# Attention and routed experts on one core: order of the value loads, the memory rows, the casts and the noise load

## The chip, the cores and the metric

The kernel runs on one core of a Trainium2 chip. A core has a matrix engine (TensorE, PE in the profile, PEld for its weight loads), a vector engine (VectorE, DVE), an activation engine (ScalarE, ACT), a general engine (GpSimd, POOL) and SyncE (SP), which here only issues transfers. Transfers are started from the instruction queues of SP, ACT and GpSimd and carried by 16 DMA engines. The metric is the time of one execution on the device in microseconds, the median of several runs.

## What is computed

Four batches of 768 tokens with 8 heads of 64 go through chunked attention: each chunk of 32 queries sees 8 memory keys and a window of 16 tokens before it, its own 32 and 8 after it. The result, 3072 rows of 512, goes through a router that picks two of eight experts for each row, with noise in the choice.

```python
for c in range(nc):
    k_full = np.concatenate([mem_k, k[:, :, l_start:r_end]], axis=2)
    v_full = np.concatenate([mem_v, v[:, :, l_start:r_end]], axis=2)
    scores = scale * np.matmul(q_c, k_full.transpose(0, 1, 3, 2))
    a = np.exp(scores - np.max(scores, axis=-1, keepdims=True))
    out[:, :, c_start:c_end] = np.matmul(a / (np.sum(a, axis=-1, keepdims=True) + 1e-09), v_full)
...
noisy_logits = x @ w_gate + np.log1p(np.exp(x @ w_noise)) * noise
top2 = np.argpartition(-noisy_logits, 2, axis=1)[:, :2]
top2_w = softmax of the two logits
out[rows of e] += top2_w * (np.maximum(x @ w1[e], 0.0) @ w2[e])
```

Inputs are float32; the kernel computes in bfloat16 with float32 sums.

## The kernel before

There are two stages. The attention stage works through 12 tiles of 256 tokens, three to a batch (`i` counts tiles, `b` batches, `tp` the tile in its batch), and routes each batch while the next one runs. The expert stage then gathers rows of equal expert pairs and runs the two matmuls of each expert (`mm1`, L645, and `mm2`, L654). All eight experts' weights live in one large SBUF tile, `w_all`; the attention stage's buffers are cut from the end of the same tile, so a row of the profile that names `w_all` may be a weight or any of these buffers, and its line tells which.

Buffers of the attention stage: `k32`, `q32` and `v32` hold one batch of float32 keys, queries and values as they are loaded; `nat` holds keys and queries in bfloat16, two batches; `vb` holds the values in bfloat16, two batches. `vb` is laid out in groups of 64 rows on each of two halves of the partitions (`a` is 0 or 1, even and odd heads): 56 rows of a window and 8 memory rows, for 13 even groups and 12 odd ones, which are the same tokens moved by 32.

The steps that the change touches, with their engines and lines:

- `fetch` (L111): one transfer by SP's queue for a batch of keys or queries, 1536 KB.
- `fetch_v` (L119, L123, L127): a batch of values, 1536 KB, in twelve transfers by SP's queue, which alternate between the halves. For batch 0 it goes in two parts, groups below `VA` = 5 and the rest.
- `narrow` (L337): keys or queries to bfloat16; by ScalarE and VectorE for batch 0, by GpSimd after that (`cp_p`, L479 in the profile).
- `cast_v` (L314): values to bfloat16 on 64 partitions, by GpSimd, except one by VectorE in batch 0.
- `shift_v` (L322, L323): two transfers by SP's queue that make a half's odd groups from its even ones.
- `memory_v` (L333 for batch 0, L330 after it): the memory rows `mvn` into eight partitions of each half, by SP's queue. It must wait until the shifts have read the places that it overwrites.
- `turns` (L346 and L473): transposes of keys (`KU`) and queries (`QU`) on TensorE with copies by ScalarE and VectorE.
- `scores` (L357 to L375), `exps` (L380), `turn_p` (L387, L390), `values` (L398 to L413), `turn_x` (L421, L423), `gate` (L433, L435): the work on a tile. `values` needs the cast groups, the shifted groups and the memory rows.
- `keep_x` (L440): the tile's rows to HBM, by GpSimd's queue for the first seven tiles, by SP's after that.
- `route` (L231 to L311): a generator of eight steps for a batch. Each `next` records one: exponentials (1), first choice (2, L240 to L251), second choice (3, L256 to L264), ranks on TensorE and `d` on GpSimd (4, L267 to L288), `vals` on GpSimd (5, L296), ranks read (6), `oh_l` (7, L304), lists (8, L308, L310).
- `load_expert`, `load_part` (L74, L75, L81, L83): expert weights by GpSimd's queue. Each waits until the buffers that it overwrites are free.

For PE, ACT, DVE and SP the order of instructions is that of the program text (`manual_schedule`). On GpSimd each instruction that is given to `pin` keeps its place. Every queue works in order: an instruction that waits holds all behind it. SP's transfers take eight semaphores in turn, so a transfer is issued only when the eighth before it has landed.

In a middle batch of the kernel before, tile 0 narrows the next batch's keys and fetches the keys after that; tile 1 does the same for queries and casts half 0 of the values; tile 2 casts half 1, and SP's queue then has the shifts, the values of the batch after next, and the memory rows, in this order:

```python
if tp == 2:
    for a in range(2):
        shift_v(b + 1, a)
    if b + 2 < B:
        fetch_v(b + 2)
    memory_v(b + 1)
```

The noise `nz` is loaded by SP's queue ahead of tile 0 (L503). The casts of the memory values `mvn` (L162) and of the gate weights `wgn` (L168) are VectorE's work before the first key transposes.

Of the kernel before, what the change touches and what calls it, by code (L numbers as in the profile page):

```python
# [22 lines left out]
def kernel(  # L23
# [14 lines left out]
    nc = tc.nc  # L38
    B, H, S, D = q.shape
    NM = mem_k.shape[2]  # L40
    CH, LC, RC = 32, 16, 8
# [28 lines left out]
    def pin(i):  # L70
        tc.keep_in_program_order(i)
# [37 lines left out]
    def fetch(x, b):  # L109
        t, a = {"k": (k32, k), "q": (q32, q)}[x]  # L110
        nc.sync.dma_start(out=t, in_=a[b].rearrange("h (p s) d -> p h (s d)", s=SO))  # L111


    def fetch_v(b, g0=0, g1=NB):
        src = [v[b].rearrange("(c a) t d -> a t c d", a=2)[a] for a in range(2)]
        t = [v32[a * 64:a * 64 + 64] for a in range(2)]
        if g0 == 0:
            for a in range(2):
                nc.sync.dma_start(out=t[a][LC:64, 0], in_=src[a][0:64 - LC])  # L119
        lo, hi = max(g0, 1), min(g1, NB - 1)  # L120
        for c in range(HP):
            for a in range(2):
                nc.sync.dma_start(out=t[a][:, lo:hi, c],  # L123
                                  in_=src[a][lo * 64 - LC:hi * 64 - LC, c].rearrange("(g p) d -> p g d", p=64))
        if g1 == NB:
            for a in range(2):
                nc.sync.dma_start(out=t[a][0:LC, NB - 1], in_=src[a][S - LC:S])  # L127


    for g in (0, NB - 1):  # L130
# [1 line left out]
    fetch("k", 0)  # L132
    fetch("q", 0)
    VA = 5
    fetch_v(0, 0, VA)

    actx = ExitStack()
    keep = actx.enter_context(tc.tile_pool(name="keep", bufs=1))
# [19 lines left out]
    mvs = wflat[0:NM, 0:2 * B * Dm].bitcast(F32).rearrange("m (b h d) -> m b h d", b=B, h=H)  # L158
    nc.scalar.dma_start(out=mvs, in_=mem_v.rearrange("b h m d -> m b h d"))
    mvn = keep.tile([NM, B, Dm], BF16, name="mvn")  # L160
    for b in range(B):
        nc.vector.tensor_copy(mvn[:, b].rearrange("m (a c d) -> m a c d", a=2, c=HP),  # L162
                              mvs[:, b].rearrange("m (c a) d -> m a c d", a=2))
    wgs = keep.tile([128, KP, 2 * E], F32, name="wgs")
    nc.scalar.dma_start(out=wgs[:, :, 0:E], in_=moe_w_gate.rearrange("(kp p) e -> p kp e", p=128))
    nc.scalar.dma_start(out=wgs[:, :, E:2 * E], in_=moe_w_noise.rearrange("(kp p) e -> p kp e", p=128))
    wgn = const.tile([128, KP, 2 * E], BF16, name="wgn")
    nc.vector.tensor_copy(wgn, wgs)  # L168
    nz = const.tile([128, NG, E], F32, name="nz")
# [143 lines left out]
    def cast_v(b, a, g0, g1, eng):  # L313
        i = eng.tensor_copy(out=vb[b % 2][a * 64:a * 64 + 64, a, g0:g1],  # L314
                            in_=v32[a * 64:a * 64 + 64, g0:g1].rearrange("p g c d -> p g (c d)"))
        if eng is nc.gpsimd:
            pin(i)


    def shift_v(b, a, g0=0, g1=NB - 1):  # L320
        t = vb[b % 2][a * 64:a * 64 + 64, a]
        nc.sync.dma_start(out=t[0:32, NB + g0:NB + g1], in_=t[32:64, g0:g1])  # L322
        nc.sync.dma_start(out=t[32:WIN, NB + g0:NB + g1], in_=t[0:WIN - 32, g0 + 1:g1 + 1])  # L323

    def memory_v(b, g0=0, g1=NB - 1):
        for a in range(2):
            t = vb[b % 2][a * 64 + WIN:a * 64 + KW, a]
            m = mvn[:, b, a * HP * D:(a + 1) * HP * D].unsqueeze(1)
            if g1 - g0 == NB - 1:
                nc.sync.dma_start(out=t, in_=m.to_broadcast([NM, 2 * NB - 1, HP * D]))  # L330
# [150 lines left out]
    with tc.manual_schedule(engines={ET.PE, ET.Activation, ET.DVE, ET.SP}):  # L481


        for x, us in ((0, KU), (1, QU)):
            narrow(x, 0, 0, cp_a)
            narrow(x, 0, 1, cp_v)
            turns(0, us, [cp_a, cp_v])
        cast_v(0, 0, 0, VA, nc.gpsimd)
        cast_v(0, 1, 0, VA, nc.vector)
        for a in range(2):  # L490
            shift_v(0, a, 0, VA - 1)
        fetch_v(0, VA)
# [12 lines left out]
        for i in range(NT):  # L505
            b, tp = divmod(i, TP)
            more, last = b + 1 < B, b + 1 == B
            r = routes.get(b - 1)
            if i:
                keep_x(i - 1, nc.gpsimd if i < NT - 4 else nc.sync)  # L510
            if tp == 2 and r:
                next(r)
            if more:
                if tp < 2:
                    for par in range(2):
                        narrow(tp, b + 1, par, cp_p)
                    if b + 2 < B:
                        fetch("kq"[tp], b + 2)
                if tp:
                    cast_v(b + 1, tp - 1, 0, 7, nc.gpsimd)  # L520
                    cast_v(b + 1, tp - 1, 7, NB, nc.gpsimd)
                if tp == 2:
                    for a in range(2):
# [6 lines left out]
            if i == NT - 4:  # L530
                load_expert(1)
            if i == NT - 3:
                load_part(2, 0)
                load_part(2, 1)
# [6 lines left out]
            if i == NT - 1:  # L541
                next(r)
                next(r)
            if i:
                xTs_[i - 1] = turn_x(xrs.pop(i - 1))
            pTs[i] = turn_p(pbs.pop(i))
            if i:
                gate(i - 1, xTs_.pop(i - 1))
            if i + 1 < NT and not held:
                pbs[i + 1] = exps(sc)  # L550

            if tp == 0 and b:
                r = routes[b - 1] = route((b - 1) * SO, SO, lgs[b - 1])
                next(r)
            if tp and r and i < NT - 1:
                next(r)
# [36 lines left out]
        src = next(dec)  # L593
# [296 lines left out]
```

## Time and profile before

| | us |
|---|---|
| median of 3 runs | 440.17 (437.24 to 440.24) |
| time of the profiled execution | 440.2 |
| its span, first to last instruction | 438.5 |
| PE busy | 304.6 |
| DVE busy | 173.7 |
| POOL busy | 150.1 |
| ACT busy | 126.8 |
| first routed rows asked for by GpSimd (L608) | 199.55 |
| expert matmuls back to back from | 216.76 |

The page's second part cuts the span into 40 slices of 11 us. Its digits are tenths of a slice in which an engine was busy; PEclk is the clock that TensorE was granted, in tenths; DMA is the mean busy share of the 16 DMA engines.

```profile
PE   0433183035717654533799999999999999999990
DVE  6563044028617563874212332167431133202230
POOL 9303436016526710236840653206152022100021
PEclk9965575556665655555899999999999999889997
DMA  8546889976481999202999997062121012100011
```

To the left of the eighteenth slice is the attention stage: no engine is busy throughout, and TensorE is nearly idle in slices 7 to 9 (66 to 99 us). To the right, from slice 20 on, TensorE is busy all the time. A row of the groups reads: line, engine, operation, output and inputs, count, then busy time and mean duration, then the idle time of the engine just before these instructions and what ended most of it.

### The profile page before, as it was taken

The numbers are of one execution on the slowest core, as the hardware profiler recorded it, in microseconds if no ns is written. First come the engines' busy times: TensorE is split into PE (matmuls) and PEld (weight loads), VectorE is DVE, ScalarE is ACT, GpSimd is POOL, SyncE is SP. The second block draws the span as 40 slices with busy tenths as digits, with TensorE's granted clock in tenths as the row PEclk, the third lists the DMA queues.
The fourth block names the chain that finished last, engine by engine and source line by source line (L and its number), as shares of the span: only waits on it lengthen the run. The fifth ranks groups of instructions, "written<-read, shape, count | busy, mean of one in ns | idle before, by whom it ended". The sixth has DMA issues, their size and how long they took to land.

```text
span 438.5 us, 7981 instructions
## 1 busy us (share of the span) xinstructions
PE 304.6 (69%) x3315; PEld 192.7 (44%) x3315; DVE 173.7 (40%) x362; ACT 126.8 (29%) x193; POOL 150.1 (34%) x180
## 2 busy tenths in 40 slices
PE   0433183035717654533799999999999999999990
PEld 0423073034606543422455544667446666445540
DVE  6563044028617563874212332167431133202230
ACT  2330153015424441310243223422224312024310
POOL 9303436016526710236840653206152022100021
PEclk9965575556665655555899999999999999889997
DMA  8546889976481999202999997062121012100011
GB/s 236 125 104 196 208 129 356 177 182 190 99 142 30 156 230 218 58 24 73 185 242 210 229 215 172 24 99 81 43 81 50 0 38 87 43 1 3 17 49 55
DMA packets 59320, 53.29 MB, mean 122 GB/s; under 512 B 32455, under 2 KB 51703, under 8 KB 59280
## 3 DMA queue, kind: packets, MB, share of 16 engines
q0 software_dynamic: 16912, 28.71, 30.6%
q1 hardware_dynamic: 40776, 23.85, 23.1%
q8 instruction: 28, 0.46, 0.4%
q10 hardware_dynamic: 1592, 0.16, 0.3%
q14 instruction: 12, 0.10, 0.1%
HBM read 56.49 MB, written 10.75 MB: 153 GB/s over the span
## 4 chain that ended last, share of the span: by engine, by line
PE 49%; DVE 3%; DMA 2%; POOL 1%; issue 1%; POOLq 0%; ACT 0%; DVEq 0%
PE p_y L654 24%; PE p_h L645 23%; DMA xt<-xd,main_src 2%; PE p_xt L626 1%; POOL xt L608 1%; DVE w_all L413 0%; DVE oh_l L304 0%; PE p_list L308 0%; PE p_x L421 0%; POOL facts L285 0%; PE ps_o L405 0%; POOLq L845 0%; DVE y L660 0%; DVE listed L310 0%; PE p_xt L760 0%
## 5 line engine op out<-in xcount | busy, mean ns | idle before, releaser
L654 PE MATMUL p_y<-w_all,h 128*128 128x512 bf16 (+1 forms) x464 | 107.0, 387 | 0.0
L645 PE MATMUL p_h<-xTt,w_all 128*128 128x384 bf16 (+2 forms) x640 | 103.1, 321 | 0.0
L645 PEld LDWEIGHTS <-w_all 128*128 128x128 bf16 (+1 forms) x704 | 68.5, 99 | 42.5 <-issue 3.7
L633 ACT ACTIVATE h<-p_h 128x512 bf16<-128x512 f32 (+1 forms) x82 | 44.7, 545 | 112.6 <-PE p_h L645 105.7
L631 DVE TENSOR_SCALAR h<-p_h 128x512 bf16<-128x512 f32 (+1 forms) x50 | 31.3, 626 | 97.0 <-PE p_h L645 90.1
L654 PEld LDWEIGHTS <-h 128*128 128x128 bf16 x464 | 45.7, 100 | 53.1 <-issue 3.8
L612 POOL DMA_INDIRECT out_dram<-y,main_dst x28 | 30.9, 1105 | 103.8 <-DVE y L660 90.4
L405 PE MATMUL ps_o<-w_all,pT 128*32 128x128 bf16 x384 | 12.4, 295 | 53.4 <-DMA w_all<-mvn 53.4
L413 DVE TENSOR_TENSOR w_all<-ps_o,rs 128x512 bf16<-128x512 f32 x24 | 15.5, 686 | 59.6 <-PE ps_o L405 59.1
L660 DVE SCALAR_TENSOR_TENSOR y<-p_y,main_w,y 128x512 f32<-128x512 f32 x28 | 21.0, 750 | 37.4 <-PE p_y L654 35.1
L608 POOL DMA_INDIRECT xt<-xd,main_src x28 | 27.4, 977 | 23.6 <-PE p_xt L626 15.4
L405 PEld LDWEIGHTS <-pT 128*32 128x32 bf16 x384 | 9.1, 131 | 54.2 <-issue 39.3
L314 POOL CAST w_all<-w_all 64x1792 bf16<-64x1792 f32 (+3 forms) x15 | 23.5, 1591 | 26.7 <-DMA w_all<-mvn 13.4
L423 ACT COPY xT<-p_x 128x1024 bf16<-128x1024 bf16 x12 | 12.2, 1015 | 69.8 <-PE p_x L421 69.8
L658 ACT ACTIVATE y<-p_y,main_w 128x512 f32<-128x512 f32 x28 | 19.2, 687 | 42.2 <-PE p_y L654 41.2
L346 PE MATMUL p_t<-identb,w_all 128*128 128x128 bf16 x192 | 20.9, 295 | 9.6 <-DVE mkT L229 3.5
L346 PEld LDWEIGHTS <-w_all 128*128 128x128 bf16 x192 | 18.3, 137 | 11.3 <-ACT w_all L337 5.7
L479 POOL CAST w_all<-w_all 128x1536 bf16<-128x1536 f32 x12 | 17.2, 1465 | 12.8 <-DMA w_all<-in_k_dram 8.0
L440 POOL DMA_DIRECT2D xd<-w_all x7 | 5.3, 763 | 41.3 <-DVE ps_s L370 35.0
L626 PE MATMUL p_xt<-identb,xt 128*128 128x128 bf16 x116 | 10.3, 235 | 8.8 <-DMA xt<-xd,main_src 8.0
L373 DVE TENSOR_REDUCE mx<-ps_s 128x16 f32<-128x1024 f32 x12 | 14.7, 1224 | 3.6 <-PE ps_s L363 3.3
L380 ACT ACTIVATE pb<-sc 128x1024 bf16<-128x1024 f32 x12 | 12.7, 1061 | 10.9 <-DVE sc L375 10.9
(160 smaller groups left out, 311.7 us busy)
## 6 DMA issues: line engine op xcount, KB each, us to landing
w_all<-in_moe_w_dram POOLq DMA_DIRECT2D x10, 1024.0 KB, 14.7
w_all<-in_k_dram SPq DMA_DIRECT2D x4, 1536.0 KB
w_all<-in_q_dram SPq DMA_DIRECT2D x4, 1536.0 KB
w_all<-in_moe_w_dram POOLq DMA_DIRECT2D x12, 512.0 KB, 8.4
w_all<-in_v_dram SPq DMA_DIRECT2D x24, 176.0 KB
xd<-w_all POOLq DMA_DIRECT2D x7, 256.0 KB, 5.0
xd<-w_all SPq DMA_DIRECT2D x5, 256.0 KB
w_all<-w_all SPq DMA_DIRECT2D x6, 192.0 KB
```

The source lines that it names most:

```text
L314: i = eng.tensor_copy(out=vb[b % 2][a * 64:a * 64 + 64, a, g0:g1], in_=v32[a * 64:a * 64 + 64, g0:g1].rearrange("p g c d -> p g (c d)"))
L346: nc.tensor.transpose(out=p_t[:, s, :], in_=src[:, pair, s, :], identity=identb)
L405: nc.tensor.matmul(out=ps_o[r * CH:(r + 1) * CH, j, 2 * pair:2 * pair + 2, :], lhsT=pT[:, j * HP + pair, r * CH:(r + 1) * CH], rhs=vb[b % ...
L479: pin(nc.gpsimd.tensor_copy(o_, i_))
L608: pin(nc.gpsimd.indirect_dma_start(out=xts[key].bitcast(I32), out_offset=None, in_=xd, in_offset=bass.IndirectOffsetOnAxis(ap=ix, axis=0)))
L612: i = nc.gpsimd.indirect_dma_start(out=out, out_offset=bass.IndirectOffsetOnAxis(ap=ix, axis=0), in_=y, in_offset=None, bounds_check=N - 1 ...
L631: nc.vector.tensor_scalar(out=out_, in0=in_, scalar1=0.0, scalar2=None, op0=Alu.max)
L633: nc.scalar.activation(out=out_, in_=in_, func=Act.Relu)
L645: nc.tensor.matmul(out=o, lhsT=w(kp * F + f * 128, 128), rhs=x[:, kp], start=(kp == 0), stop=(kp == KP - 1))
L654: nc.tensor.matmul(out=p, lhsT=h[:, (f * n + j) * 128:(f * n + j + 1) * 128], rhs=w(KP * F + f * Dm, Dm), start=(f == 0), stop=(f == FB - 1))
L658: nc.scalar.activation(out=y, in_=p, func=Act.Copy, scale=weight)
L660: nc.vector.scalar_tensor_tensor(out=y, in0=p, scalar=weight, in1=y, op0=Alu.mult, op1=Alu.add)
```

## The change

The values of the next batch are cast at tile 1 of batch 0 and at tile 0 of every later batch, both halves together, instead of over tiles 1 and 2. The queue of SP then has the shifts, a load of keys or queries, the memory rows, and only after them the values of the batch after next. Values are fetched one half after the other. In batch 0 the memory rows of the first part stand between the two halves of the second part of the values, and those of the second part behind the keys of batch 1 but in front of the queries. Narrowing of keys and queries and their fetches move by about a tile. In `route`, the second choice (3) comes behind the tile's values, `vals` (5) follows at tile 1, and the ranks and `oh_l` (6, 7) come ahead of the next scores. Expert weights are asked for one tile later. The noise goes by GpSimd's queue at the start; the casts of `mvn` and `wgn` move behind the first value cast and the first scores.

```diff
-    def fetch_v(b, g0=0, g1=NB):
-        src = [v[b].rearrange("(c a) t d -> a t c d", a=2)[a] for a in range(2)]
-        t = [v32[a * 64:a * 64 + 64] for a in range(2)]
+    def fetch_v(b, a, g0=0, g1=NB):
+        src = v[b].rearrange("(c a) t d -> a t c d", a=2)[a]
+        t = v32[a * 64:a * 64 + 64]
...
-    for b in range(B):
-        nc.vector.tensor_copy(mvn[:, b].rearrange("m (a c d) -> m a c d", a=2, c=HP),
-                              mvs[:, b].rearrange("m (c a) d -> m a c d", a=2))
...
-    nc.vector.tensor_copy(wgn, wgs)
     nz = const.tile([128, NG, E], F32, name="nz")
+    pin(nc.gpsimd.dma_start(out=nz, in_=moe_noise.rearrange("(g p) e -> p g e", p=128)))
...
-        for x, us in ((0, KU), (1, QU)):
-            narrow(x, 0, 0, cp_a)
-            narrow(x, 0, 1, cp_v)
-            turns(0, us, [cp_a, cp_v])
+        narrow(0, 0, 0, cp_a)
+        narrow(0, 0, 1, cp_v)
+        turns(0, KU, [cp_a, cp_v])
+        narrow(1, 0, 0, cp_a)
+        narrow(1, 0, 1, cp_v)
+        turns(0, QU, [cp_v, cp_a])
         cast_v(0, 0, 0, VA, nc.gpsimd)
         cast_v(0, 1, 0, VA, nc.vector)
+        for b in range(B):
+            nc.vector.tensor_copy(mvn[:, b].rearrange("m (a c d) -> m a c d", a=2, c=HP),
+                                  mvs[:, b].rearrange("m (c a) d -> m a c d", a=2))
         for a in range(2):
             shift_v(0, a, 0, VA - 1)
-        fetch_v(0, VA)
+        fetch_v(0, 0, VA)
         memory_v(0, 0, VA - 1)
-        fetch("k", 1)
+        fetch_v(0, 1, VA)
+        pbs[0] = exps(scores(0))
+        nc.vector.tensor_copy(wgn, wgs)
         for a in range(2):
             cast_v(0, a, VA, NB, nc.gpsimd)
-        pbs[0] = exps(scores(0))
+            shift_v(0, a, VA - 1)
+        fetch("k", 1)
+        memory_v(0, VA - 1)
+        fetch("q", 1)
         for a in range(2):
-            shift_v(0, a, VA - 1)
-        fetch("q", 1)
-        memory_v(0, VA - 1)
-        fetch_v(1)
-        nc.sync.dma_start(out=nz, in_=moe_noise.rearrange("(g p) e -> p g e", p=128))
+            fetch_v(1, a)
+        for par in range(2):
+            narrow(0, 1, par, cp_p)
         routes = {}
         for i in range(NT):
...
+            if more and tp == min(b, 1):
+                for par in range(2):
+                    narrow(1, b + 1, par, cp_p)
+                if b == 0:
+                    fetch("k", 2)
+                elif b + 2 < B:
+                    fetch("q", b + 2)
+            if more and tp == 1 - min(b, 1):
+                for a in range(2):
+                    cast_v(b + 1, a, 0, 7, nc.gpsimd)
+                    cast_v(b + 1, a, 7, NB, nc.gpsimd)
+                    shift_v(b + 1, a)
+                if b + 2 < B:
+                    fetch("k" if b else "q", b + 2)
+                memory_v(b + 1)
+                if b + 2 < B:
+                    for a in range(2):
+                        fetch_v(b + 2, a)
+            if b + 2 < B and tp == 2:
+                for par in range(2):
+                    narrow(0, b + 2, par, cp_p)
+            if i == NT - 4:
+                load_expert(0)
+            if i == NT - 3:
+                load_expert(1)
+            if i == NT - 2:
+                load_part(2, 0)
+                load_part(2, 1)
             if tp == 2 and r:
                 next(r)
-            if more:
-                if tp < 2:
-                    for par in range(2):
-                        narrow(tp, b + 1, par, cp_p)
-                    if b + 2 < B:
-                        fetch("kq"[tp], b + 2)
-                if tp:
-                    cast_v(b + 1, tp - 1, 0, 7, nc.gpsimd)
-                    cast_v(b + 1, tp - 1, 7, NB, nc.gpsimd)
-                if tp == 2:
-                    for a in range(2):
-                        shift_v(b + 1, a)
-                    if b + 2 < B:
-                        fetch_v(b + 2)
-                    memory_v(b + 1)
-            if i == NT - 5:
-                load_expert(0)
...
+                next(r)
...
-            if tp and r and i < NT - 1:
-                next(r)
+            if tp == 1 and r:
                 next(r)
...
             xrs[i] = values(i, pTs.pop(i))
+            if tp == 1 and r:
+                next(r)
             if tp == 1 and more:
                 turns(b + 1, KU, [cp_a])
+            if tp == 1 and r:
+                next(r)
+                next(r)
...
-            if tp and r and i < NT - 1:
+            if tp == 2 and r and not last:
                 next(r)
```

More of the change, by code (lines that the diff above doesn't have):

```diff
@@ L111, in fetch @@
         nc.sync.dma_start(out=t, in_=a[b].rearrange("h (p s) d -> p h (s d)", s=SO))
-    def fetch_v(b, g0=0, g1=NB):
-        src = [v[b].rearrange("(c a) t d -> a t c d", a=2)[a] for a in range(2)]
-        t = [v32[a * 64:a * 64 + 64] for a in range(2)]
+    def fetch_v(b, a, g0=0, g1=NB):
+        src = v[b].rearrange("(c a) t d -> a t c d", a=2)[a]
+        t = v32[a * 64:a * 64 + 64]
         if g0 == 0:
-            for a in range(2):
-                nc.sync.dma_start(out=t[a][LC:64, 0], in_=src[a][0:64 - LC])
+            nc.sync.dma_start(out=t[LC:64, 0], in_=src[0:64 - LC])
         lo, hi = max(g0, 1), min(g1, NB - 1)
         for c in range(HP):
-            for a in range(2):
-                nc.sync.dma_start(out=t[a][:, lo:hi, c],
-                                  in_=src[a][lo * 64 - LC:hi * 64 - LC, c].rearrange("(g p) d -> p g d", p=64))
+            nc.sync.dma_start(out=t[:, lo:hi, c],
+                              in_=src[lo * 64 - LC:hi * 64 - LC, c].rearrange("(g p) d -> p g d", p=64))
         if g1 == NB:
-            for a in range(2):
-                nc.sync.dma_start(out=t[a][0:LC, NB - 1], in_=src[a][S - LC:S])
+            nc.sync.dma_start(out=t[0:LC, NB - 1], in_=src[S - LC:S])
     for g in (0, NB - 1):
@@ L134 @@
     VA = 5
-    fetch_v(0, 0, VA)
+    for a in range(2):
+        fetch_v(0, a, 0, VA)
     actx = ExitStack()
@@ L510 @@
                 keep_x(i - 1, nc.gpsimd if i < NT - 4 else nc.sync)
+            if more and tp == min(b, 1):
[14 more added lines that the diff above has]
+                if b + 2 < B:
+                    for a in range(2):
+                        fetch_v(b + 2, a)
[9 more added lines that the diff above has]
+                load_part(2, 1)
             if tp == 2 and r:
                 next(r)
-            if more:
-                if tp < 2:
-                    for par in range(2):
-                        narrow(tp, b + 1, par, cp_p)
-                    if b + 2 < B:
-                        fetch("kq"[tp], b + 2)
-                if tp:
-                    cast_v(b + 1, tp - 1, 0, 7, nc.gpsimd)
-                    cast_v(b + 1, tp - 1, 7, NB, nc.gpsimd)
-                if tp == 2:
-                    for a in range(2):
-                        shift_v(b + 1, a)
-                    if b + 2 < B:
-                        fetch_v(b + 2)
-                    memory_v(b + 1)
-            if i == NT - 5:
-                load_expert(0)
[L530 to L534, printed above, removed]
+                next(r)
             held = i == TP - 1
@@ L540 @@
                 sc = scores(i + 1)
-            if i == NT - 1:
-                next(r)
-                next(r)
             if i:
```

1 line of the change is left out of this document (removed).

## The prediction

> **What bounds the kernel now.** The profiled execution has a span of 438.5 us and a time of 440.2, so 1.7 us lie outside the span; the median of the three runs is 440.17, and the sum below is made against 440.2. I read the chain that ended last first: from 216.8 us to 428 it is matmuls of the expert stage back to back, which the change does not touch. Before that it goes through the gather of rows and the routing of the last batch, so the expert stage begins when the attention stage ends, and what the attention stage waits for counts in full. The page's costliest groups name that wait:
>
> ```profile
> L654 PE MATMUL p_y<-w_all,h 128*128 128x512 bf16 (+1 forms) x464 | 107.0, 387 | 0.0
> L645 PE MATMUL p_h<-xTt,w_all 128*128 128x384 bf16 (+2 forms) x640 | 103.1, 321 | 0.0
> ...
> L405 PE MATMUL ps_o<-w_all,pT 128*32 128x128 bf16 x384 | 12.4, 295 | 53.4 <-DMA w_all<-mvn 53.4
> ```
>
> The two expert lines wait for nothing. The values matmul (L405) works 12.4 us and waits 53.4, all of it for the memory rows (mvn). TensorE's timeline shows where, namely at the first values of each batch, and at tile 1:
>
> ```profile
> 36.21 0.29 PE L405 MATMUL ps_o<-w_all,pT 128*32 128x128 bf16 x1 [5.65 <-DMA w_all<-mvn]
> ...
> 53.96 0.27 PE L405 MATMUL ps_o<-w_all,pT 128*32 128x128 bf16 x1 [8.30 <-DMA w_all<-mvn]
> ...
> 94.27 1.04 PE L405 MATMUL ps_o<-w_all,pT 128*32 128x128 bf16 x32 [20.63 <-DMA w_all<-mvn]
> ...
> 132.88 1.04 PE L405 MATMUL ps_o<-w_all,pT 128*32 128x128 bf16 x32 [9.91 <-DMA w_all<-mvn]
> ...
> 170.01 1.16 PE L405 MATMUL ps_o<-w_all,pT 128*32 128x128 bf16 x32 [8.02 <-DMA w_all<-mvn]
> ```
>
> I call these five starts T0, T1, T3, T6 and T9 after their tiles. Why the rows come late stands in SP's queue ahead of T3:
>
> ```profile
> 70.48 0.78 SPq L323 DMA_DIRECT2D w_all<-w_all  x1
> 71.32 1.05 SPq L119 DMA_DIRECT2D w_all<-in_v_dram  x2
> 72.41 13.14 SPq L123 DMA_DIRECT2D w_all<-in_v_dram  x8
> 85.59 1.54 SPq L127 DMA_DIRECT2D w_all<-in_v_dram  x2
> 87.18 1.54 SPq L330 DMA_DIRECT2D w_all<-mvn  x2
> ```
>
> The shifts of batch 1 are issued by 71.3, but its memory rows only at 87.2, behind twelve transfers of batch 2's values. The same stands ahead of T6 (values 116.3 to 126.3, rows at 126.4). At T9 no load is left to queue behind; there the rows land beside expert weights.
>
> **Prices of the transfers.** Stretches with one kind of transfer (last two columns: DMA share, GB/s):
>
> ```profile
> 81.00:87.00 6.00, 0.00 (x0) 0.00 (x0) 0.00 (x0) 0.00 (x0) 0.00 (x0) 0.50 1.17 174
> 103.00:106.00 3.00, 0.00 (x0) 0.00 (x0) 2.65 (x11) 0.88 (x2) 0.86 (x3) 0.50 1.03 383
> 128.00:132.00 4.00, 0.00 (x0) 0.00 (x0) 0.00 (x0) 0.00 (x0) 0.00 (x0) 0.50 0.34 44
> 116.00:118.00 2.00, 1.73 (x44) 1.45 (x44) 1.84 (x5) 0.93 (x1) 0.00 (x0) 0.50 0.83 183
> ```
>
> So one batch costs the engines: values, 1536 KB at 174 GB/s, 9.0 us; keys or queries, 1536 KB at 383, 4.1 each; memory rows, 200 KB at 44, 4.7; the shifts, 336 KB per half at 183, 1.8 a half. Transfers of SP go through in the order of issue, as the row of 87.2 shows, and SP keeps eight in flight at most (they take eight semaphores in turn).
>
> **The change, part by part.**
>
> *T0.* VectorE's cast of the gate weights (L168) now stands behind the first scores; before, VectorE idled 3.0 us in front of it, with the key copies behind. The query load's landing takes the place of part of this: I take 2 us of the 3. Shift a=1 then ends at 23.9 instead of 25.9. Five value transfers instead of ten (5.40 + 1.08, halved: 3.2) come before the first memory rows: 27.1. Issuing those takes 3.0, and 1.4 to land (35.5 to 36.97 before): 31.6 for the second half, 31 for the first matmul. The mvn casts (four, 1.72) go onto VectorE behind the value cast and end by 26, under SP's issuing; without that cover T0 would be 1.7 later.
>
> The noise load goes from SP to GpSimd's queue at about 10 us. GpSimd is idle from 13.1 to 19.3, so its issue costs nothing (one to two us bound it, by the 0.7 to 0.9 of its other DMAs). Its 96 KB took 62 to 65 us on the engines, at 44 GB/s; I count between 0 and 3 us on the first loads, take 1, and T0 is 32. The Trainium skill ("DMA: Bandwidth & Descriptors", section "Issuing engines are not separate DMA queues") says that queues of different engines share the DMA engines and interleave, and that only issue time is saved; by it alone the 3 us would move rather than go, and the sum would be 2 us higher. The trace shows the queues sharing the DMA engines (195 GB/s in all where expert weights and rows ran together), not this move.
>
> *T1.* Five value transfers (3.2) end at 35; the second half lands at 35.5, its GpSimd cast (1.92) ends at 37.5, its shift's issue (1.55) at 39, keys of batch 1 at 39.5. The rows must wait for the shifts to land and come behind the keys (4.1): they land at 46. Before, keys and queries both were in front, and T1 was 54.
>
> *T3.* Now it is a row of transfers from 46: queries 4.1, values of batch 1 9.0, keys of batch 2 4.1, shifts 3.6, queries of batch 2 4.1, rows 4.7: 29.6, hence T3 = 75 instead of 94.3. TensorE would be ready for it at about 66 (queries narrowed on GpSimd at 52, turned, and 12.1 us from the values of tile 2 to those of tile 3 as before), so some 9 of the 20.6 us of waiting remain: T3 has its load of values out of the way, not its keys and queries.
>
> *T6.* Behind the rows come batch 2's values (9.0): 84. GpSimd now casts them ahead of keep_x and of the queries of batch 2: cast a=1 (3.09) 87.1, keep_x 0.75, narrow (2.87) 90.7. Queued behind this on GpSimd are the routing's d and vals; TensorE waits for the narrow with its query turns. From those to T6 it was 108.06 to 132.88 less 9.91, that is 14.9: T6 = 105.6. Its rows: shift 88.7, keys 4.1, rows 4.7, landed at 98, so that no wait is left. Compute alone gives 75 + 28.7 = 103.7; I take 105.6.
>
> *T9.* Compute from T6 was 37.1 less 8.02, 29.1: 134.7. Supply: values of batch 3 at 107, cast 110, queries 111.5, narrow 114.5, plus 14.9 is 129.4. TensorE decides, T9 = 134.7 instead of 170.0, 35.3 earlier.
>
> *Behind T9.* Same work as before (270.2 us). The expert loads (L74, L75, L81) move by one or two tiles and now start near 120 in one row; they took 143 to 177 before, so they end near 154, ahead of the gather at 164. If that cover were gone, the first expert matmul would wait, up to 10 us. The routing's reordered VectorE steps do the same work; the two-input ones can stall beside GpSimd:
>
> ```profile
> L240 DVE TENSOR_TENSOR nl<-ns,nz x5: 174/199/4195, 99.5 to 192.4; 128x48 f32<-128x48 f32 x3, 128x32 f32<-128x32 f32 x1, 128x16 f32<-128x16 f32 x1
> ```
>
> 199 ns as a rule, 4.2 us twice (99.5 and 138.1), each time until GpSimd's casts were through. I leave both stalls in.
>
> Sum: 440.2 - 35.3 = 405, own range 397 to 412.
>
> **Rivals.**
>
> *More goes.* The stalls of 4 us vanish in batches 1 and 2, for the value casts leave that place, and T3 comes 4 us earlier with rows and keys overlapping: 405 - 8 - 4 = 393. For it: only the query narrow (2.87) still stands beside L240. Against: GpSimd's cast wait moves the narrow to just there.
>
> *GpSimd and VectorE collide more.* Per batch the casts (6.2) and the narrow (2.9) now come in one stretch; if all 9 us fell on two-input steps in place of 4, and in front of T6 and T9, that is 2 x 5: 415. The Trainium skill ("GPSIMD Engine Reference", section "Key points") says that GpSimd shares its SBUF interfaces with VectorE and contends with instructions of two SBUF inputs; by that rule this is the outcome, and the two rows of 4.2 us agree with it.
>
> *Little changes.* The rows still stand behind keys or queries, and a late cast only exchanges the wait: only T0 and T1 gain, 8 us, 432. Against it: 9.0 us of values leave the row ahead of both T3 and T6.
>
> *Slower.* The halves (64 partitions each) now go one after the other instead of by turns. If a half fills the engines no better than the eight-partition rows (44 GB/s, share 0.34), values take 36 us, not 9. They stand once in the supply row ahead of each of T3, T6 and T9, so T9 becomes 129 + 3 x 27 = 210 and the time 480. It decides for slower from 23 us a batch (68 GB/s). Against: the 32-partition shifts already reach 183.
>
> **Chances and range.** Forecast 0.60, more 0.17, collision 0.12, little 0.06, slower 0.05. A measurement of this kernel can tell about 1% (4.4 us) from no change. All but the last are faster by more; of "little" I give 0.02 to within 1%. So 0.93 faster, 0.02 same, 0.05 slower. The range runs from 393 to 419, over forecast, more and collision and 4 us past that for the noise load and the half loads.
>
> **What would show it.** In the changed profile L405's waits should fall from 53.4 to some 20 us, with T0, T1, T3, T6, T9 near 32, 46, 75, 106, 135, no wait at T6 and T9, and SP's L330 row ahead of the value loads. Values landing later than 84 us for batch 2, query turns waiting over 5 us for GpSimd, or an expert matmul waiting for weights would make it wrong.

## The result and the profile after

| | before | after |
|---|---|---|
| median | 438.71 (436.45 to 440.24, 4 runs) | 422.22 (421.15 to 425.15, 4 runs) |
| profiled execution, its span | 440.2, 438.5 | 423.0, 421.3 |
| first routed rows asked for by GpSimd | 199.55 | 180.74 |

The ratio is 0.9639, 95% interval 0.9565 to 0.9712: the changed kernel is faster, by 17.2 us in the profiled executions where 35.3 were forecast. The time lies outside the forecast's range of 393 to 419.

The page's costliest groups of the changed kernel (TensorE's values matmul is now L400):

```profile
L309 POOL CAST w_all<-w_all 64x1792 bf16<-64x1792 f32 (+3 forms) x15 | 23.5, 1589 | 46.0 <-DMA w_all<-in_v_dram 46.0
...
L400 PE MATMUL ps_o<-w_all,pT 128*32 128x128 bf16 x384 | 12.9, 295 | 28.0 <-DMA w_all<-mvn 26.3
```

The values matmul waits 28.0 us instead of 53.4, but GpSimd's value casts (L309), which are asked for earlier now, wait 46.0 us for the values. In the kernel of before these casts (L314 there) waited 26.7 us:

```profile
L314 POOL CAST w_all<-w_all 64x1792 bf16<-64x1792 f32 (+3 forms) x15 | 23.5, 1591 | 26.7 <-DMA w_all<-mvn 13.4
```

The wait has partly changed its engine. The expert matmuls (L657, L666) still wait for nothing. TensorE's timeline, first values of each batch and tile 1:

```profile
30.92 0.26 PE L400 MATMUL ps_o<-w_all,pT 128*32 128x128 bf16 x1 [0.99 <-DMA w_all<-mvn]
...
49.38 1.39 PE L400 MATMUL ps_o<-w_all,pT 128*32 128x128 bf16 x32 [11.42 <-DMA w_all<-mvn]
...
83.94 1.17 PE L400 MATMUL ps_o<-w_all,pT 128*32 128x128 bf16 x32 [13.41 <-DMA w_all<-mvn]
...
116.49 1.04 PE L400 MATMUL ps_o<-w_all,pT 128*32 128x128 bf16 x32
...
148.79 0.63 PE L400 MATMUL ps_o<-w_all,pT 128*32 128x128 bf16 x32
```

| | T0 | T1 | T3 | T6 | T9 | gather | end |
|---|---|---|---|---|---|---|---|
| before | 36.2 | 54.0 | 94.3 | 132.9 | 170.0 | 199.6 | 440.2 |
| forecast | 32 | 46 | 75 | 105.6 | 134.7 | 164.2 | 405 |
| after | 30.9 | 49.4 | 83.9 | 116.5 | 148.8 | 180.7 | 423.0 |
| after less forecast | -1.1 | +3.4 | +8.9 | +10.9 | +14.1 | +16.5 | +18.0 |

No wait is left in front of T6 and T9, as forecast, and still they are 11 and 14 us late. The delay grows with each batch. SP's queue shows one cause, here from the second half of batch 2's values to the rows behind them:

```profile
85.69 3.45 SPq L121 DMA_DIRECT2D w_all<-in_v_dram  x4
89.19 0.93 SPq L124 DMA_DIRECT2D w_all<-in_v_dram  x1
92.45 0.59 SPq L317 DMA_DIRECT2D w_all<-w_all  x1
93.09 0.85 SPq L318 DMA_DIRECT2D w_all<-w_all  x1
97.19 0.55 SPq L317 DMA_DIRECT2D w_all<-w_all  x1
97.78 0.78 SPq L318 DMA_DIRECT2D w_all<-w_all  x1
98.60 0.93 SPq L111 DMA_DIRECT2D w_all<-in_k_dram  x1
99.64 2.02 SPq L325 DMA_DIRECT2D w_all<-mvn  x2
```

The values of batch 2 are all issued at 90.1. The next entries are the shifts (L317, L318). Each waits for GpSimd's cast of its half, which waits for the landing, so between 90.1 and 98.6 the queue issues nothing else; keys (L111) and rows (L325) stand behind. What the DMA engines did meanwhile (last two columns: DMA share, GB/s):

```profile
96.00:98.00 2.00, 0.00 (x0) 0.00 (x0) 1.86 (x5) 0.00 (x0) 1.95 (x3) 0.50 0.00 0
```

Nothing at all. From one half-1 shift to the next (69.47, 97.19, 127.86) a batch took 27.7 and 30.7 us, where the forecast's supply row has 25.5.

### The profile page after: what moved, and what is told of

Its sections match the earlier page's. It is cut to its first block, busy times and chain, and to the rows that moved or that the text cites. A ratio compares the mean times of both kernels' runs of the same rounds, so it can differ in the third digit from the quotient of the medians.

```text
span 421.3 us, 7988 instructions
## 1 busy us (share of the span) xinstructions
PE 306.9 (73%) x3315; PEld 195.0 (46%) x3315; DVE 175.8 (42%) x362; ACT 126.5 (30%) x193; POOL 151.2 (36%) x181
## 4 chain that ended last, share of the span: by engine, by line
PE 55%; DMA 17%; SPq 13%; POOL 4%; issue 3%; DVE 3%; ACT 3%; POOLq 0%; DVEq 0%; ACTq 0%
PE p_y L666 25%; PE p_h L657 24%; SPq L121 10%; DMA w_all<-in_q_dram 6%; DMA w_all<-in_v_dram 4%; DMA xt<-xd,main_src 2%; DMA w_all<-w_all 2%; DMA w_all<-in_k_dram 2%; POOL w_all L309 1%; PE p_xt L638 1%; SPq L124 1%; PE p_x L416 1%; PE ps_o L400 1%; ACT pT L385 1%; ACT xT L418 1%
## 5 line engine op out<-in xcount | busy, mean ns | idle before, releaser
L666 PE MATMUL p_y<-w_all,h 128*128 128x512 bf16 (+1 forms) x464 | 107.2, 388 | 0.0
L657 PE MATMUL p_h<-xTt,w_all 128*128 128x384 bf16 (+2 forms) x640 | 103.5, 321 | 0.0
L657 PEld LDWEIGHTS <-w_all 128*128 128x128 bf16 (+1 forms) x704 | 68.4, 99 | 42.7 <-issue 4.5
L666 PEld LDWEIGHTS <-h 128*128 128x128 bf16 x464 | 45.6, 99 | 53.3 <-issue 4.0
L624 POOL DMA_INDIRECT out_dram<-y,main_dst x28 | 30.9, 1105 | 103.9 <-DVE y L672 90.4
L309 POOL CAST w_all<-w_all 64x1792 bf16<-64x1792 f32 (+3 forms) x15 | 23.5, 1589 | 46.0 <-DMA w_all<-in_v_dram 46.0
L672 DVE SCALAR_TENSOR_TENSOR y<-p_y,main_w,y 128x512 f32<-128x512 f32 x28 | 21.0, 750 | 37.4 <-PE p_y L666 32.3
L620 POOL DMA_INDIRECT xt<-xd,main_src x28 | 27.3, 977 | 23.7 <-PE p_xt L638 15.7
L400 PE MATMUL ps_o<-w_all,pT 128*32 128x128 bf16 x384 | 12.9, 295 | 28.0 <-DMA w_all<-mvn 26.3
L341 PEld LDWEIGHTS <-w_all 128*128 128x128 bf16 x192 | 19.7, 146 | 12.9 <-ACT w_all L332 7.1
L400 PEld LDWEIGHTS <-pT 128*32 128x32 bf16 x384 | 9.2, 130 | 29.2 <-DMA w_all<-mvn 25.2
L263 PE MATMUL p_rank<-ohp,tri 128*128 128x168 bf16 (+2 forms) x5 | 1.4, 274 | 20.9 <-DVE ohp L259 20.9
L375 ACT ACTIVATE pb<-sc 128x1024 bf16<-128x1024 f32 x12 | 12.7, 1061 | 10.9 <-DVE sc L370 10.9
```

Of the source, the lines that this page charges most:

```text
L341: nc.tensor.transpose(out=p_t[:, s, :], in_=src[:, pair, s, :], identity=identb)
L400: nc.tensor.matmul(out=ps_o[r * CH:(r + 1) * CH, j, 2 * pair:2 * pair + 2, :], lhsT=pT[:, j * HP + pair, r * CH:(r + 1) * CH], rhs=vb[b % ...
L620: pin(nc.gpsimd.indirect_dma_start(out=xts[key].bitcast(I32), out_offset=None, in_=xd, in_offset=bass.IndirectOffsetOnAxis(ap=ix, axis=0)))
L624: i = nc.gpsimd.indirect_dma_start(out=out, out_offset=bass.IndirectOffsetOnAxis(ap=ix, axis=0), in_=y, in_offset=None, bounds_check=N - 1 ...
L657: nc.tensor.matmul(out=o, lhsT=w(kp * F + f * 128, 128), rhs=x[:, kp], start=(kp == 0), stop=(kp == KP - 1))
L666: nc.tensor.matmul(out=p, lhsT=h[:, (f * n + j) * 128:(f * n + j + 1) * 128], rhs=w(KP * F + f * Dm, Dm), start=(f == 0), stop=(f == FB - 1))
```

## The experiments

Times are medians. Ratios are to the kernel of before, measured in the same series, with their 95% intervals. The marks T0 to T9 are those of one profiled execution. Two executions of one kernel can differ there: e4 and e13 below are the same program, and their T3 is 82.4 and 85.2, their T9 146.0 and 149.2. The changed kernel and its repeat e12 lie closer (83.9 and 83.1, 148.8 and 148.9).

**Which edit brings the gain.** e1 is the kernel of before with two entries of SP's queue swapped:

```diff
+                    memory_v(b + 1)
                     if b + 2 < B:
                         fetch_v(b + 2)
-                    memory_v(b + 1)
```

> The kernel before with one edit: in a middle batch the memory rows are issued before the next values instead of after them. If the place of the rows in SP's queue carries the gain, most of it is here: the values of tile 3 start near 86 us instead of 94, those of tile 6 near 116 instead of 133, and the time is 418 to 426. If it needs the casts a batch ahead, the wait only moves to the values' casts, and the time stays above 432.

Measured: 421.69, 0.9642 (0.9602 to 0.9683), T3 85.5, T6 116.0, T9 155.2. The swap alone gives the whole gain of the changed kernel; all its other edits together net to nothing. (e1's profiled execution is the slowest of its five, 425.7, so its marks may be some us late.)

e11 is the changed kernel's start, halves and routing with the main loop of before, rows first:

> The changed kernel with the main loop's narrowing, casts, fetches and weight loads of the kernel before, the memory rows ahead of the next values; the start, the load by half and the routing order stay as changed. If casting a batch ahead is worth nothing beside the place of the rows, this is within 3 us of 422. If it gives the 4 us that tiles 6 and 9 no longer wait, this is 424 to 430. If it costs by holding the query turns behind the casts, 414 to 419.

Measured: 421.16, 0.9580 (0.9541 to 0.9618). Its T0 and T1 are 30.8 and 49.0 against e1's 35.7 and 54.0, its T3 85.2 against 85.5: the 5 us won at the start are gone by T3. The new main loop, with its casts a batch ahead, is worth nothing net.

e2 fetches whole batches of values with alternating halves, as before:

> The changed kernel with the whole-batch value loads issued by turns to the two halves, as before. If a half by itself loads slowly (144 GB/s between 52 and 57 us in the changed kernel, 174 by turns before), the values of batch 1 land 2 to 3 us earlier, and the time falls to 414 to 419. If the halves are not the cause, the first cast has to wait longer for its half and the second as long as it does now: 421 to 428.

Measured: 422.10, 0.9640 (0.9573 to 0.9707), T3 85.0. The order of the halves has no effect on the time.

e3 puts the steps of `route` where they were:

> The changed kernel with the routing's steps recorded in the order of the kernel before. If the reordering is worth nothing, 420 to 425. If the two-input steps beside the casts cost what their longer durations suggest (some 7 us in batch 1), the old order has them at the same place but with the tile's division behind them, so that it is 1 to 4 us slower: 423 to 427.

Measured: 421.29, 0.9647 (0.9598 to 0.9696). T6 is 4.3 us later (120.8), T9 only 0.6 (149.4), and from T9 to the gather it takes 29.6 us instead of 31.9. What the reordering wins in the middle is gone by T9, and behind T9 it costs 2.3; the medians are the same. The 2.3 is more than chance: from T9 to the gather the kernel of before, e1 and e9, with the old order, take 29.5 or 29.6 too, the repeats e12 and e13 with the new one 31.9.

e4 moves the noise back to SP's queue, behind the values of batch 1; e12 and e13 repeat the changed kernel and e4 side by side:

```diff
-    pin(nc.gpsimd.dma_start(out=nz, in_=moe_noise.rearrange("(g p) e -> p g e", p=128)))
...
             fetch_v(1, a)
+        nc.sync.dma_start(out=nz, in_=moe_noise.rearrange("(g p) e -> p g e", p=128))
```

> The changed kernel with the noise loaded by SP's queue behind the values of batch 1, as before. If its 3 us on the DMA engines lie in the supply row that sets the time, the values of tile 3 start 2 to 3 us later and the time is 424 to 427. If that row has slack there, or the early load costs as much in front of the first values, 420 to 423.

> The changed kernel once more, beside the next one on the same chip: 420 to 424.

> The changed kernel with the noise by SP's queue once more. If the noise by GpSimd's queue costs, 2 to 4 us below the changed kernel in the same call; if the 3 us seen before were spread between runs, within 1.5 us of it.

Measured: e4 418.86, 0.9582 (0.9540 to 0.9624); e12 422.14, 0.9608 (0.9566 to 0.9650); e13 420.09, 0.9554 (0.9524 to 0.9585). With the noise by SP the kernel was 2.1 us faster in the pair e12 and e13, 3.2 against e2 (the changed kernel but for the halves) in the first series and 0.6 in a third pair (e7 against e5, below). The intervals overlap in each pair, so: not a gain, probably a loss of about 2 us.

**What the supply row is made of.** Five kernels leave out or put off one kind of transfer. Their whole times are not compared, since what they leave out changes the choice of experts (e8 and e16 run some 5700 matmuls instead of 3315 and take over 940 us). What is read is T3, T6, T9 and the casts. e8 leaves out half 0 of the values of batches 1 to 3:

> The changed kernel without the loads of half 0 of the values of batches 1 to 3 (4.5 us of transfers a batch at 174 GB/s are left out; casts, shifts and rows stay). If the transfers' volume sets the supply row, tile 3 comes 4 to 5 us earlier and tiles 6 and 9 at least as much: 412 to 417. If it is the chain of hops, load, cast, shift, landing, rows, only a part of that shows: 417 to 422.

Measured: T3 79.0, T6 107.3, T9 134.9, that is 5.0, 9.2 and 13.9 earlier, for 4.5 us of transfers a batch. So in the changed kernel supply sets the stage all the way, and at T3 the value bytes count at about the price that the forecast took. T3 to T6 and T6 to T9 are 28.3 and 27.6 here, and TensorE waits for no transfer in them: that is the work of a batch alone, so what these two batches save, 4.2 and 4.7, is bounded by it.

Four more have one execution each. e14 puts the writes of x off, e15 leaves out keys and queries of batches 2 and 3, e16 the memory rows and e17 the shifts of those batches:

> The changed kernel, with the writes of x (256 KB each) of tiles 0 to 8 put off to the last tile, where all nine go in one row with stale contents; only the attention stage up to T9 can be read. In the changed kernel half 1 of the value casts ends at 69.5, 97.2 and 127.8, and T3, T6, T9 are 83.9, 116.5, 148.8 (repeat: 83.1, 115.3, 148.9). If these writes are the term that the supply row left out (1.4 us each at the 183 GB/s of the shifts, 4.2 a batch): T3 2 to 4 us earlier, T6 5 to 8, T9 9 to 12. If they only fill gaps that the hops leave: all within 1.5 us.

> The changed kernel without the loads of keys and queries of batches 2 and 3 (the batch before the last in the same buffer is read again); only the attention stage can be read. At their undisturbed price (4.1 us each) two of them ahead of T3: T3 at 75 to 77; from there the work of a batch decides, 28 us as in the run without half of the values: T6 104, T9 132. If transfers that run side by side cost more than their sum (queries of batch 3 land 10.5 us after issue, keys 11.7): T3 at 72 or earlier. If keys and queries are hidden beside the casts and hops: T3 at 81 or later.

> The changed kernel without the memory rows of batches 2 and 3 (those of batches 0 and 1 stay in the buffers); only the attention stage can be read. T3 unchanged within 1.5 us. If the rows count at their price in the supply row (4.7 us): casts of half 1 of batch 3 end about 4.7 earlier (123), T6 about the same to 1 us earlier, since batch 2 does not wait for its rows, T9 4 to 5 earlier. If rows share the engines with keys and values without lengthening them: all within 1.5 us.

> The changed kernel without the shifts of batches 2 and 3 (those of batches 0 and 1 stay in the buffers); only the attention stage can be read. T3 unchanged. At the price of the supply row (3.6 us a batch): casts of half 1 of batch 3 end at about 124 instead of 127.8 and T9 3 to 4 earlier. If the hop costs its latency too (half 1 issued at 97.2, landed 3.7 later with the engines idle from 96 to 98): 120 or earlier, T9 6 or more earlier. If the hop is covered by the keys: within 1.5 us.

Ends of the half-1 casts of batches 2 and 3 on GpSimd, and the start of SP's half-1 value loads of batch 3 (L121), less those of the changed kernel (97.2, 127.8, 114.7):

| left out | in the row, up to batch 3 | cast, batch 2 | cast, batch 3 | loads issued | T9 |
|---|---|---|---|---|---|
| writes of x (e14) | not counted | -1.3 | -3.1 | -3.4 | -3.1 |
| keys, queries (e15) | 8.2, then 12.3 | -5.6 | -13.3 | -11.7 | -10.8 |
| rows (e16) | 4.7 | +1.0 | -2.8 | -1.3 | -1.8 |
| shifts (e17) | 3.6 | -0.1 | -8.2 | -10.9 | -5.3 |

How much of this is chance: e4 and e13, one kernel, differ by 1.6 to 1.7 us in these casts and loads and by 3.1 at T9. Keys and queries save 5.6 where two of them (8.2) stand ahead of batch 2's values, and 13.3 where three (12.3) stand ahead of batch 3's. What the rows save can't be told well: 2.8 at one cast, the rest within the spread. The writes of x, which the row left out, save some 3 us over two batches at the cast and the loads. The shifts alone clearly save more than their price: SP's queue is 10.9 us earlier for one batch's shifts of 3.6 us. (Two further numbers of e17 are bounded by something else: its cast of batch 3 found the values already there, and T9 is then set by TensorE and VectorE.) The windows of e17 over the same 2 us:

```profile
96.00:98.00 2.00, 0.00 (x0) 0.00 (x0) 1.86 (x5) 0.00 (x0) 1.95 (x3) 0.71 0.76 223
```

The engines work there at a share of 0.76, with keys (issued at 90.4) and rows (from 92.2) that no longer stand behind a shift.

**The queue's standstill, with all work in.** If it is the standstill and not the shifts' own transfer, it is enough to put the load of keys or queries ahead of the shifts:

```diff
             if more and tp == 1 - min(b, 1):
+                if b + 2 < B:
+                    fetch("k" if b else "q", b + 2)
                 for a in range(2):
...
                     shift_v(b + 1, a)
-                if b + 2 < B:
-                    fetch("k" if b else "q", b + 2)
```

> The changed kernel with the load of the next but one batch's queries (batch 0) or keys (batches 1 and 2) ahead of the shifts instead of behind them; nothing is left out. If SP's queue standing still at the shift until the cast has ended is what the supply row missed: the engines move 1536 KB in that gap, the rows go behind the shift at once, half 1 of batch 3's values is cast by 121 to 125 instead of 127.8, T9 3 to 5 us earlier, and the ratio to the kernel of before is 0.950 to 0.957. If the transfer of the shifts itself is the term, or the keys only take the landing of the shifts with them: the same as the changed kernel (0.9608, 422) within 1.5 us; if the shifts now land behind 1536 KB, T3 is 3 us later.

Measured: 418.62 (417.14 to 419.37), 0.9520 (0.9477 to 0.9563), against the changed kernel's 0.9608 (0.9566 to 0.9650) in another series; the two intervals just miss each other. SP's queue and the window of 96 to 98 us in e18:

```profile
90.84 1.54 SPq L111 DMA_DIRECT2D w_all<-in_k_dram  x1
92.49 0.86 SPq L317 DMA_DIRECT2D w_all<-w_all  x1
...
98.52 0.55 SPq L317 DMA_DIRECT2D w_all<-w_all  x1
...
100.74 2.16 SPq L325 DMA_DIRECT2D w_all<-mvn  x2
```

```profile
96.00:98.00 2.00, 0.00 (x0) 0.00 (x0) 1.97 (x3) 0.00 (x0) 2.00 (x2) 0.50 1.03 359
```

The keys now run through the gap, at 359 GB/s where there were none. The shift of half 1 is 1.3 us later and the rows 1.1 (100.74 instead of 99.64), and yet the half-1 cast of batch 3 ends at 122.3 instead of 127.8 and T9 is 145.5 instead of 148.8. The 5.5 at the cast is well outside the spread; the 3.3 at T9 by itself would hardly be. T6 to T9 takes 28.4 us, the work of a batch alone. T3 did not move (83.6). There the move has a price too: with the queries ahead of it the shift of half 1 of batch 1 lands 9.8 us after its issue at 68.87, where it took 5.1 in the changed kernel (by the chains of waits of the two), and the first rows, which wait for it, are issued at 77.0 instead of 72.4.

**GpSimd and VectorE.** e5 narrows the queries at tile 0, ahead of the value casts, and fetches the next ones there; e7 is e5 with the noise by SP:

```diff
-            if more and tp == min(b, 1):
+            if more and tp == 0:
```

> The changed kernel with one condition edited: from batch 1 on the queries are narrowed on GpSimd at tile 0, ahead of the value casts, and the next queries are fetched there too. If the query turns' wait for GpSimd, which stands behind the casts in the changed kernel (narrow ends at 100.8 and 134.4 us), is what keeps tiles 5 and 8 late, their values start near 104 and 134 us instead of 110.1 and 142.5, and the time falls to 410 to 415. If the supply of values sets those tiles, the queries fetched earlier push them back and the time stays within 3 us of 422.

> The kernel with queries narrowed ahead of the casts, and the noise loaded by SP's queue behind the values of batch 1. If the early noise load costs 3 us in front of the first tiles, as 418.9 against 422.2 says, and both act in different places, this is 3 us below the run without it: 407 to 412. If the two overlap, 410 to 415.

Measured: e5 417.25, 0.9538 (0.9471 to 0.9605); e7 416.65, 0.9523 (0.9453 to 0.9593). By the medians a gain of some 5 us on the changed kernel, about half of what was expected; the intervals overlap. A second wait is still there. TensorE's ranks (L263, L268 in e1) wait for VectorE's `ohp`: 7.8 us in the changed kernel, 6.6 in e5, 1.9 in e1. The changed kernel and e1:

```profile
101.20 0.32 PE L263 MATMUL p_rank<-ohp,tri 128*128 128x168 bf16 x1 [7.83 <-DVE ohp L259]
```

```profile
95.53 0.25 PE L268 MATMUL p_rank<-ohp,tri 128*128 128x168 bf16 x1 [1.86 <-DVE ohp L264]
```

In e1 the casts are spread over two tiles. VectorE's timeline of the changed kernel shows what it does ahead of `ohp`:

```profile
89.24 0.20 DVE L235 TENSOR_TENSOR nl<-ns,nz 128x48 f32<-128x48 f32 x1
89.47 1.61 DVE L236 TENSOR_TENSOR nl<-nl,lg 128x48 f32<-128x48 f32 x1
...
94.42 1.38 DVE L251 TENSOR_TENSOR nl<-desc,ii 128x48 f32<-128x48 f32 x1
95.84 1.38 DVE L252 SCALAR_TENSOR_TENSOR nl<-nl,nl 128x48 f32<-128x48 f32 x1
```

The same kind of step takes 0.20 us alone and 1.4 to 1.6 while GpSimd casts (89.35 to 92.43 and 94.07 to 97.16; it narrows from 97.88 on). Six such steps, with those of 1.1 to 1.3 at 91.35, 98.21 and 99.46, take 8.0 us ahead of the ranks, 6.8 more than at 0.20 each.

**Two that brought little.** e9 is e1 with the expert weights a tile later; e10 is e7 with keys and queries of batches 1 to 3 by ScalarE's queue:

> The kernel before with two edits: memory rows ahead of the next values, and expert weights asked for one tile later. The first alone left 12.8 us of waiting at tile 9, where the rows land beside the weights. If the weights are the cause of that wait, it falls to 4 to 8 us and the time to 413 to 418; if the rows are late by themselves, the wait and the time (421.7) stay.

> The kernel with queries narrowed first and the noise by SP (416.7), with the keys and queries of batches 1 to 3 loaded by ScalarE's queue instead of SP's. If the order within SP's one queue and its eight transfers in flight hold the memory rows back, the rows no longer stand behind keys and queries and tile 3 starts 4 to 8 us earlier: 405 to 412. If the volume on the DMA engines sets the supply, as the run with half of the values says, tile 3 stays within 2 us of 83 and the time within 3 of 416.7.

Measured: e9 418.79, 0.9591 (0.9535 to 0.9648); T9's wait fell from 12.8 to 8.4 us. e10 420.47, 0.9564 (0.9515 to 0.9613), no gain over e7: ScalarE's own copy at 46.7 us stood 20.3 us behind a blocked load, and T0 came at 48.1. So e10 doesn't tell what a free queue would have given.

**The best version.** e19 is e7 with e18's move:

> The best version so far (queries narrowed first, noise by SP; 0.9523) with the same move. If the gap at the shift counts there too: 0.940 to 0.947, some 412 to 415 us. If not: 0.950 to 0.955.

Measured: 414.66 (413.37 to 416.43), 0.9430 (0.9386 to 0.9475). It beats the kernel of before by 5.7% and, across series, the changed one by some 7.5 us. The medians look as if the two gains added (0.9523 + 0.9520 - 0.9608 = 0.9435), but that is not shown: the intervals of e7 and e19 overlap, and the first routed rows are asked for at 177.0 in e7's profile and at 176.6 in e19's.

## Why the prediction was right and wrong

*The bound and the mechanism: right.* The wait of the values matmul for the memory rows was the bound, and the rows' place in SP's queue the cause; e1 shows that by itself.

*T0: right.* 30.9 for 32. The steps by themselves give 31; the 1 us put on top for the noise can't be told from the spread (e4 and e13, with the noise elsewhere, start at 29.6 and 30.8). But what is won at the start is not carried on: e11 against e1.

*T1: 3.4 us late.* The load of keys was issued at 39.7 (39.5 forecast), and narrowing could begin only at 47.9, 8.2 us later, where the row has 4.1; the rows behind the keys landed at 49.4. While the queue stood at the shifts ahead, the engines had run down (changed kernel, columns as above):

```profile
35.00:39.00 4.00, 1.48 (x23) 1.30 (x22) 2.06 (x4) 2.69 (x3) 1.89 (x1) 0.50 0.29 66
39.00:42.00 3.00, 0.00 (x0) 0.00 (x0) 0.00 (x0) 0.00 (x0) 0.00 (x0) 0.50 0.67 135
42.00:46.00 4.00, 0.00 (x0) 0.00 (x0) 0.00 (x0) 0.00 (x0) 0.00 (x0) 0.50 1.04 363
```

At 42 to 46 the keys run at nearly the forecast's rate. The time is lost before they start and, as far as these windows tell, between their last byte and GpSimd.

*T3, the step that failed: "a row of transfers from 46: queries 4.1, values of batch 1 9.0, keys of batch 2 4.1, shifts 3.6, queries of batch 2 4.1, rows 4.7: 29.6".* T1 to T3 took 34.6. Most of the difference lies in the first two terms: from T1 (49.4) to the landing of batch 1's values (66.2) it took 16.8 us, where the row has 13.1. The engines did not stand still there (a share of 1.31, and 1.12 from 57 to 70 us); the values moved more slowly than the 174 GB/s of the price:

```profile
52.00:57.00 5.00, 3.98 (x64) 3.69 (x65) 0.43 (x3) 4.43 (x6) 1.48 (x2) 0.72 1.31 144
```

Why they did is open; with the old order of the halves (e2) T3 was no earlier. The writes of x were left out of the row (some 3 us over two batches, e14). (46 and 29.6 make 75.6; the forecast went on with 75.)

*The same sum, one batch on: no gap between transfers.* The row lets transfers follow each other without a gap, and for the batches behind T3 that is what failed. A shift waits for a cast, the cast for a landing, and SP's in-order queue stands at the shift meanwhile. The forecast priced the shifts at 3.6 us a batch; e17 measured 10.9 of SP's queue, and e18 recovers 5.5 at the cast of batch 3 by filling the gap. That is shown for the gap of batch 2. For the 5 us between T1 and T3 it is not: e18's move there left T3 at 83.6. The standstill could have been seen ahead of the change. SP's own waits in the kernel of before have it, 19.8 us in six waits, the longest 9.7 (in the changed kernel 20.1 in eight):

```profile
SPq L322 <- POOL w_all L314: 19.8, 6, 9.7
```

*T6, 2.0 us more than the 30.6 from T3 forecast.* The path was the forecast one: values of batch 2 landed 9.8 us after T3 (9.0), cast and narrow followed in 7.0 (6.7), and from there to T6 it took 15.7 (14.9). No wait for rows, as said. The narrowing ended at 100.8, but on TensorE the query turns stand behind the ranks, whose `ohp` came at 101.2, so that they began at 102.0. One of the prediction's own signs of being wrong was there: the values of batch 2 landed at 93.8, not by 84. "I leave both stalls in" was about right in sum: the two stalls of 4.2 us are gone, but many of 1.1 to 1.6 took their place. The Trainium skill ("GPSIMD Engine Reference", section "Key points") says that GpSimd shares its SBUF interfaces with VectorE and contends with instructions of two SBUF inputs; the rows of VectorE above agree, with 0.20 us against 1.4 to 1.6. The rival built on it was right in kind, not in size: of its 10 us, e5 got back about 5, by medians whose intervals overlap.

*T9, forecast as TensorE's: wrong.* "Compute from T6" of 29.1 was the right size (28.4 in e18), but in the changed kernel supply decided, with 32.3. Its queries were issued at 120.1 (115.3 in e18) and landed at 130.6, their narrowing ended at 134.4, and T9 came 14.4 us behind that (14.9 forecast); the forecast had the narrowing ready at 114.5, out of the same gapless sum. With the gap filled (e18) the work decides.

*Behind T9: "same work as before", 4.0 us wrong.* To the gather 2.4 more, which e3 puts down to the new order of the routing (29.6 with the old). The other 1.6 us are in the expert stage and lie within its spread: from the gather to the end it takes 240.6 before and 242.3 after, 243.0 in the repeat e12, and 239.6 and 241.2 in e4 and e13, one kernel. The expert weights were asked for at 137.8 instead of near 120 and were in time all the same.

*The noise, "take 1" as its cost, a gain against before.* It landed 9.3 us after its issue and did not pay: e4, e7 and e13 are 0.6 to 3.2 us faster without the move, by medians whose intervals overlap. The Trainium skill ("DMA: Bandwidth & Descriptors", section "Issuing engines are not separate DMA queues") says that such a move saves issue time only; these runs agree in that no gain shows.

*The rivals.* "Slower", by half loads that fill the engines badly, is refuted by e2. "Little changes" gave too little but named what happened: a late cast exchanges the wait, here for GpSimd's 46.0 us on values. "More goes" did not come.

## What to carry to other kernels

A sum of undisturbed transfer times was a lower bound for this queue, not a forecast: for each entry that waits for an engine, add the chain from landing over the engine's work to the next issue, and look whether the DMA engines have anything to do meanwhile. In an in-order queue, put independent loads in front of the transfer that waits, not behind it, but look at what waits for that transfer: it lands behind their bytes (e18, 9.8 us at batch 1, and nothing won at T3). When a change has many edits, run the smallest one by itself: here two swapped entries were the whole gain.

## What the runs showed of the hardware

A transfer of a few hundred KB costs more than its bytes: the two shifts of half 1, 1.8 us by rate, landed 5.1 us after the first one's issue at 69.47, with keys under way, and 3.7 after that at 97.19, with idle engines ahead of them, by the chain of waits of the changed kernel:

```profile
69.47 5.06 DMA w_all<-w_all
...
97.19 3.70 DMA w_all<-w_all
```

Keys and queries of 1536 KB, 4.1 us by rate, reached the waiting engine 8.1 and 10.5 us after their issue where other transfers were in flight (39.68 and 120.11 in the same chain). In e18, behind the keys and queries of batch 2, such a pair took 9.8. Short VectorE steps with two inputs took five to eight times as long beside GpSimd's casts (1.1 to 1.6 us against 0.20).
